# The start of a four-layer attention and gated-MLP kernel: row 0 centred first, row 1's statistics on ScalarE, and three loads moved

## The chip, the cores and the metric

One core of a Trainium2 chip. The kernel is one program, launched once; the metric is its device time in microseconds (us), the median of several runs. A profile of one execution lies beside the times. Its engines are PE (TensorE: matmuls; PEld are its weight loads), DVE (VectorE), ACT (ScalarE), POOL (GpSimd) and SP (SyncE, which here only issues DMAs). "L462" is line 462 of the kernel.

## The reference

The input x has 2048 rows of 576 numbers in bf16. Four residual layers run in turn, A, B, A, B, with the same weights each time:

```
def A(x):                                  # x is already layer-normalised
    q, k, v = split(x @ wqkv)              # 32 heads of 18
    logits = q[s] . k[s - 2 w], w = 0..7   # eight earlier rows, two apart; rows before 0 are masked
    return concat(softmax(logits * 18 ** -0.5) . v) @ wo

def B(x):
    z = gelu(x @ w_in)                     # 576 -> 4608
    z1, z2 = z[:, :2304], layernorm(z[:, 2304:])
    return (z1 * (w_sp @ z2 + b_sp[:, None])) @ w_out

x = x + A(layernorm(x));  x = x + B(layernorm(x));  x = x + A(layernorm(x));  x = x + B(layernorm(x))
```

A layernorm here subtracts the mean of a row and divides by the root of its variance plus 1e-5; it has no weights. Only the start of the first layer A is touched by the change.

## The kernel before

The rows are held in 16 tiles of 128, called rows 0 to 15 below as in the change's name (even and odd positions of the sequence are dealt out to two halves, so that a window's rows are neighbours). For the projections every normalised tile is needed transposed, in `xnT` (128 partitions, 5 chunks of the 576 columns, 2048 rows).

`layer_A` (lines 381 to 939) has a hand order: under a manual schedule the engines PE, ACT, DVE, POOL and SP take their instructions in the order in which the program writes them. For the first layer the start is lines 676 to 817:

- Loads: row 0 on SP and row 1 on ACT's queue, then on SP rows 2 and 3, the weights of v in two halves (`load_wv`), rows 4 to 7, the weights of k and q (`load_wqk`: k first, then q, then k's last 64 columns), and rows 8 to 11, which lie in a spare part of `oT`. Row tiles 12 to 15 follow later (`x3`, line 768), in a buffer that rows 0 to 3 had.
- Before the data is there: a table load for the exponential on ACT, an identity matrix, 46 matmuls on it ("warm"), small constant tables for the attention window (`build_window_rows`, lines 118 to 189), the ones in the last column of `v_ext` (line 703, ACT) and constant borders (`setup_bufs`, POOL).
- Rows 0 to 3, one after the other (lines 750 to 766): statistics on DVE (`B_` two partial statistics, `G_` the aggregate), 1/sqrt in two steps (`R_`: epsilon added on DVE, power on POOL), normalisation on DVE (`A_`), five transposes on PE and a copy by ACT to `xnT` (`T_pe`), and v projections `VW(t, half)`: five matmuls into one PSUM bank, evacuated by ACT into `v_ext`. Attention tile t begins 8 rows ahead of 128 + 120 (t - 1), so tile 1 needs the last 8 rows of row tile 0, tile 2 needs row tiles 1 and 2, tile 3 row tiles 2 and 3.
- Rows 4 to 11 are normalised in groups and transposed by DMA (`T_`, on SP's queue). The window table is written to memory in three small DMAs (`rows[2]` on SP, `rows[3]` on POOL) and read back into `win_pat` by four (`load_pat`, on SP). `fill_window_rows` spreads it over the free partitions of `QK`.
- The first half of the q and k projections (lines 788 to 793): ten steps, (d, cc) with d = 0 to 4 for cc = 0 and again for cc = 1, each with k and q (q alone for d = 4, which holds both). One unit is five matmuls of 512 columns (`PG_mm`, line 462) into one bank, evacuated by ACT into a staging buffer; a full buffer is copied by DMA into `QK` on POOL's and SP's queues. cc = 0 needs rows 0 to 3, cc = 1 rows 4 to 7.
- v projections of tiles 4 to 7, four more units, then the attention steps: logits `L_mm` (line 536), exponential, `PV` (line 559).

Banks of PSUM are taken in turn from a ring of five ("Y", "Y", "PT", "PT", "PT"); one tile more or less moves all that follow by one bank.

Of the kernel before, what the change touches and what calls it, by code (L numbers as in the profile page):

```python
# [18 lines left out]
P = 128  # L19
D = 576  # L20
H = 32
# [42 lines left out]
class K:  # L64
# [131 lines left out]

    def fill_window_rows(self, QK, half):
        nc, n = self.nc, self.cfg.S // 2
        for g0 in (0, 4):
            for a in range(2):  # L200
                nc.vector.tensor_copy(out=QK[:, a, g0:g0 + 4, half * n:(half + 1) * n].rearrange("p g (k x) -> p g k x", x=P),
                                      in_=self.pat[:, a, half, None, None, :].to_broadcast([P, 4, n // P, P]))
            if half == 0:
                nc.vector.tensor_copy(out=QK[:, :, g0:g0 + 4, 0:8], in_=self.pat0[:, :, None, :].to_broadcast([P, 2, 4, 8]))
# [176 lines left out]
    def layer_A(self, li):  # L381
# [46 lines left out]
        def k0_(t):  # L428
            return cfg.tiles[t][2]
# [16 lines left out]

        def VW(t, hh, dve):
            nk = tdim(t)[0]
            pv = self.PT_tile([P, 512], f32, "pv")
            for c in range(5):  # L450
                nc.tensor.matmul(pv[:nk, 0:288], lhsT=self.xnT[:, c, k0_(t):k0_(t) + nk],  # L451
                                 rhs=wv_sb[:, c, hh * 288:(hh + 1) * 288], start=(c == 0), stop=(c == 4))
            evac(v_ext[:nk, t, 16 * hh:16 * hh + 16, 0:DH], pv[:nk, 0:288].rearrange("p (b d) -> p b d", d=DH), dve)

# [221 lines left out]
        if li == 0:  # L676
# [20 lines left out]
            warm = self.PT_tile([P, 512], f32, "warm")  # L697
            for _ in range(46):
                nc.tensor.matmul(warm[:, 0:P], lhsT=self.ident[:], rhs=self.ident[:], start=True, stop=True)
# [3 lines left out]
            nc.scalar.copy(out=v_ext[:, :, :, DH:DH + 1], in_=self.ones[:, None, None, :].to_broadcast([P, NT, H, 1]))  # L703
# [16 lines left out]
            def S_(*tiles):  # L720
                for i in tiles:
                    B_(i)
                    G_(i)

            def R_(i0, n):
                rs = rstds[:, i0:i0 + n]
                nc.vector.tensor_scalar_add(out=rs, in0=mvs[:, i0:i0 + n, 1], scalar1=EPS)
                nc.gpsimd.tensor_tensor(out=rs, in0=rs, in1=self.neg_half[:, 0:1].to_broadcast([P, n]), op=ALU.pow)
            xns = {}
# [7 lines left out]

            def T_pe(i):
                xn = xns.pop(i)
                pt = self.PT_tile([P, 5, P], bf16, "pt")  # L740
                for c in range(5):
                    nc.tensor.transpose(pt[:, c, :], xn[:, c * P:(c + 1) * P], self.ident[:])
                r = i * P
                for c0, c1 in ((0, 3), (3, 5)) if i == 0 else ((0, 5),):
                    nc.scalar.copy(out=self.xnT[:, c0:c1, r:r + P], in_=pt[:, c0:c1])  # L745
# [16 lines left out]
            VW(2, 0, False)  # L762
            T_pe(3)
# [6 lines left out]
            S_(4, 5)  # L770
            R_(4, 2)
            A_(4, 5)
            T_(4, 5)
            S_(6, 7)
            R_(6, 2)
            rows[3](nc.gpsimd)
            A_(6, 7)
            T_(6, 7)
            S_(8)
            self.load_pat(nc.sync)  # L780
            S_(9, 10, 11)
            R_(8, 4)
            S_(12)
            A_(8, 9, 10, 11)
            T_(8, 9, 10, 11)
            self.fill_window_rows(QK, 0)
            S_(13, 14, 15)
# [481 lines left out]
```

## Time and profile before

| | |
|---|---|
| three runs | 1152.56, 1152.94, 1154.53 us; median 1152.94 |
| profiled execution | 1152.74 us, span 1150.9 us |
| PE busy | 1142.6 us of the span |
| DVE, ACT, POOL busy | 539.7, 370.5, 259.6 us |
| first projection matmul (L462) | 13.42 us |
| granted clock of PE | 1.00 throughout |

The profile's page gives the busy time of each engine, the chain of work that ended last, and groups of instructions with the mean duration of one in ns. The timeline gives start, duration, engine, line, operation, what is written from what, and in brackets the idle time before and what ended it; a "q" behind an engine's name is its queue, that is, an issue of a DMA. The view by stretches gives for each stretch the busy time and number of instructions of PE, PEld, DVE, ACT and POOL, then the granted clock, the busy share of the 16 DMA engines and GB/s. Instructions of one engine are pipelined, so neighbours can overlap by some tenths of a us.

### The profile page before, as it was taken

The numbers are of one execution on the slowest core, as the hardware profiler recorded it, in microseconds if no ns is written. First come the engines' busy times: TensorE is split into PE (matmuls) and PEld (weight loads), VectorE is DVE, ScalarE is ACT, GpSimd is POOL, SyncE is SP. The second block draws the span as 40 slices with busy tenths as digits, with TensorE's granted clock in tenths as the row PEclk, the third lists the DMA queues.
The fourth block names the chain that finished last, engine by engine and source line by source line (L and its number), as shares of the span: only waits on it lengthen the run. The fifth ranks groups of instructions, "written<-read, shape, count | busy, mean of one in ns | idle before, by whom it ended". The sixth has DMA issues, their size and how long they took to land.

```text
span 1150.9 us, 29693 instructions
## 1 busy us (share of the span) xinstructions
PE 1142.6 (99%) x12930; PEld 614.5 (53%) x12949; DVE 539.7 (47%) x1198; ACT 370.5 (32%) x660; POOL 259.6 (23%) x387
## 2 busy tenths in 40 slices
PE   8999999999999999999999999999999999999998
PEld 5567554444444444457755775544444444444676
DVE  8789987312233222244466889843322223222312
ACT  5589565011111111102247876541111111011000
POOL 3689654000000000002153767530000000000000
PEclk9999999999999999999999999999999999999999
DMA  8877696000000000049455867920000000001322
GB/s 195 183 164 200 141 211 137 10 13 13 13 1 13 13 13 2 1 152 213 110 110 110 180 152 176 246 60 1 13 13 13 13 13 1 13 2 30 101 74 58
DMA packets 177372, 91.26 MB, mean 79 GB/s; under 512 B 128788, under 2 KB 170420, under 8 KB 177242
## 3 DMA queue, kind: packets, MB, share of 16 engines
q1 hardware_dynamic: 164762, 70.75, 28.1%
q0 software_dynamic: 5888, 12.72, 4.6%
q10 hardware_dynamic: 6592, 5.90, 1.7%
q8 instruction: 101, 1.65, 0.6%
q14 instruction: 29, 0.24, 0.1%
HBM read 35.46 MB, written 14.69 MB: 44 GB/s over the span
## 4 chain that ended last, share of the span: by engine, by line
PE 97%; ACT 1%; DVE 1%; issue 0%; DVEq 0%; ACTq 0%
PE hh L234 79%; PE pp L462 6%; PE pv L451 3%; PE pw L629 3%; PE O_ps L559 3%; PE L_ps L536 2%; ACT P_sb L545 1%; PE L_ps L462 1%; PE hh L1191 0%; PE pt L595 0%; DVE ln_st L715 0%; DVE ln_xn L735 0%; DVE win_bits L158 0%; ACT v_ext L445 0%; ACT xnT L745 0%
## 5 line engine op out<-in xcount | busy, mean ns | idle before, releaser
L234 PE MATMUL hh<-Wq,Z 64*128 64x512 bf16 x4608 | 505.8, 376 | 0.0
L234 PEld LDWEIGHTS <-Z 64*128 64x128 bf16 x6984 | 339.8, 94 | 310.1
L1095 DVE TENSOR_TENSOR g_tmp<-hh,ln_xn 128x512 f32<-128x512 f32 x144 | 92.8, 686 | 452.3 <-PE hh L234 452.3
L947 ACT COPY bank_turn<-ones 1x1 bf16<-1x1 bf16 x239 | 44.8, 188 | 538.5 <-PE hh L234 538.5
L78 POOL DMA_DIRECT2D wout<-in_B_w_out_dram x4 | 4.3, 1075 | 602.0 <-PE hh L234 602.0
L234 PE MATMUL hh<-wout,Z 64*128 64x288 bf16 x2232 | 137.0, 283 | 0.0
L545 ACT ACTIVATE P_sb<-L_ps 128x1440 bf16<-128x1440 f32 (+3 forms) x136 | 125.0, 971 | 24.6 <-PE L_ps L536 23.2
L234 PE MATMUL hh<-xnT,w 64*128 64x512 bf16 x1152 | 132.2, 376 | 0.0
L234 PE MATMUL hh<-win2a,xnT 64*128 64x512 bf16 (+1 forms) x960 | 118.7, 355 | 0.0
L234 PEld LDWEIGHTS <-xnT 64*128 64x128 bf16 x1440 | 69.9, 94 | 70.0 <-issue 0.5
L1020 DVE BATCH_NORM_STATS2 z_st<-zp 128x6 f32<-128x512 bf16 (+1 forms) x160 | 93.0, 624 | 13.0 <-ACT zp L1018 12.9
L1086 ACT ACTIVATE z1T<-hh 128x1024 bf16<-128x1024 f32 x72 | 73.7, 1024 | 61.9 <-PE hh L234 61.9
L234 PEld LDWEIGHTS <-w 64*128 64x128 bf16 x1152 | 56.1, 94 | 68.3
L1096 DVE TENSOR_TENSOR Z<-g_tmp,z1T 128x512 bf16<-128x512 f32 x144 | 92.4, 683 | 0.0
L1018 ACT ACTIVATE zp<-hh 128x1024 bf16<-128x1024 f32 (+1 forms) x96 | 76.1, 810 | 48.8 <-PE hh L234 48.6
L462 PE MATMUL pp<-xnT,wqk_sb 128*128 128x512 bf16 (+1 forms) x313 | 74.2, 379 | 0.9
L234 PE MATMUL hh<-win2b,xnT 64*128 64x512 bf16 (+1 forms) x480 | 72.8, 355 | 0.0
L1160 DVE TENSOR_TENSOR x_new<-hh,xo 128x288 bf16<-128x288 f32 x64 | 26.3, 453 | 93.0 <-PE hh L234 85.0
L299 POOL TENSOR_SCALAR ln_xn<-x_new,ln_mv,ln_rstd 128x576 bf16<-128x576 bf16 x28 | 64.2, 2293 | 2.7
L78 POOL DMA_DIRECT2D QK<-stg x76 | 48.0, 636 | 36.5 <-DVE stg L443 21.9
L462 PEld LDWEIGHTS <-wqk_sb 128*128 128x128 bf16 (+1 forms) x360 | 32.1, 97 | 36.6 <-issue 1.9
L1044 POOL TENSOR_SCALAR Z<-zp,z_mv,z_rstd 128x256 bf16<-128x256 bf16 x32 | 50.7, 1584 | 3.5
(124 smaller groups left out, 753.3 us busy)
## 6 DMA issues: line engine op xcount, KB each, us to landing
xres<-x_new SPq DMA_DIRECT2D x44, 144.0 KB
wout<-in_B_w_out_dram POOLq DMA_DIRECT2D x4, 1296.0 KB, 7.4
xo<-xres SPq DMA_DIRECT2D x32, 144.0 KB
xn_rows<-ln_xn SPq DMA_DIRECT2D x28, 160.0 KB
w<-in_B_w_in_dram SPq DMA_DIRECT2D x16, 256.0 KB
QK<-stg POOLq DMA_DIRECT2D x51, 72.0 KB, 4.4
QK<-stg SPq DMA_DIRECT2D x37, 72.0 KB
xo<-in_A_x_dram SPq DMA_DIRECT2D x6, 288.0 KB
```

The lines of the kernel that those rows point to most:

```text
L78: return eng.dma_start(out=out, in_=in_)
L234: ins = self.nc.tensor.matmul(outs[a_], lhsT=lhs(a_, c, r0), rhs=rhs(a_, c, r0), start=start and k_ == 0, stop=stop and k_ == len(chunks) ...
L299: e.tensor_scalar(out=xn[:nrows, 0:D], in0=x_t[:nrows, :], scalar1=mv[:nrows, 0:1], scalar2=rstd[:nrows, 0:1], op0=ALU.subtract, op1=ALU.mult)
L462: nc.tensor.matmul(pp, lhsT=w, rhs=self.xnT[r0:r1, c, cc * 512:(cc + 1) * 512], start=start, stop=stop, tile_position=(r0, 0))
L545: nc.scalar.activation(out=P_bufs[2 * jp + s % 2][:nk, :, :, 0:nq], in_=Lv[:nk, :, :, 0:nq], func=ACT.Exp, scale=scale)
L947: self.turn_on = lambda tok: nc.scalar.copy(out=tok, in_=self.ones[0:1, 0:1])
L1018: nc.scalar.activation(out=zp[:, w0:w0 + n], in_=pz, func=ACT.Gelu_apprx_tanh)
L1020: nc.vector.bn_stats(out=st[:, x // 512, :], in_=zp[:, x:x + min(512, w0 + n - x)])
L1044: eng.tensor_scalar(out=Z[:, b0:b1, i, :], in0=zv[:, b0:b1, :], scalar1=mv[:, 0:1], scalar2=rstd[:, 0:1], op0=ALU.subtract, op1=ALU.mult)
L1086: lambda ht, z1T=z1T, q2=q2: nc.scalar.activation(out=z1T[:, q2 * 512:(q2 + 2) * 512], in_=ht[:].rearrange("p a b -> p (a b)"), func=ACT.G ...
L1095: nc.vector.tensor_tensor(out=tmp[:], in0=pg[:, a_, :], in1=bsp[:, qs], op=ALU.add)
L1096: nc.vector.tensor_tensor(out=uT(jj)[:, sub, qs], in0=tmp[:], in1=z1Ts[jj, sub][:, qs], op=ALU.mult)
```

## The change

It has these parts.

- Row 0 is centred (mean subtracted, on DVE) right after its statistics, without waiting for 1/sqrt. The centred tile is transposed into a buffer of its own (`o_slots[0]`), and both halves of v's tile 0 are projected from it; ACT multiplies by 1/sqrt when it evacuates them. Row 0 is also normalised and transposed as before, for the rest; its copy to `xnT` is split into the last 8 rows and the first 120.
- Row 1's statistics come from two passes on ACT with an accumulated sum (sum, then squared distance from the mean), with the small steps between them on POOL.
- `VW` is split into its matmuls and its evacuation, and the order on PE becomes: centred row 0, v(0,0), row 0, row 1, v(0,1), v(1,0), row 2, v(1,1), v(2,0), row 3, v(2,1), v(3,0), v(3,1).
- 30 warm matmuls in place of 46; the ones of `v_ext` by POOL, after the power of rows 6 and 7; `setup_bufs`, the clearing of `win_pat` and the write of the first-row table at other places of POOL's order.
- The load of rows 12 to 15 stands on SP behind the transposes of rows 4 to 7.
- `load_pat` is issued by ACT after the first four units of the projections; the fill is split in two, with the normalisation of rows 8 to 11 between, and the statistics of rows 12 to 15 behind.

The diff, cut:

```
-            for _ in range(46):
+            for _ in range(30):
...
-            nc.scalar.copy(out=v_ext[:, :, :, DH:DH + 1], in_=self.ones[:, None, None, :].to_broadcast([P, NT, H, 1]))
             rows[0]()
-            rows[1]()
-            setup_bufs(nc.gpsimd)
...
+            def scaled(out, in_):
+                nc.scalar.activation(out=out, in_=in_, func=ACT.Identity, scale=rstds[:, 0:1])
+            sums = sb.tile([P, 2], f32, name="lnx_sum", tag="lnx_sum", bufs=1)
+            spill = self.xn_bufs[1][:, 0:D]
+            nc.scalar.activation(out=spill, in_=xts[1], func=ACT.Identity, accum_out=sums[:, 0:1])
+            nc.gpsimd.tensor_scalar(out=mvs[:, 1, 0:1], in0=sums[:, 0:1], scalar1=1.0 / D, scalar2=None, op0=ALU.mult)
+            nc.scalar.activation(out=spill, in_=xts[1], func=ACT.Square, scale=-1.0, bias=mvs[:, 1, 0:1],
+                                 accum_out=sums[:, 1:2])
             S_(0)
-            R_(0, 1)
-            for i in range(3):
-                B_(i + 1)
-                A_(i)
-                G_(i + 1)
-                R_(i + 1, 1)
-                T_pe(i)
-                for t, hh in (((0, 0),), ((0, 1),), ((1, 0), (1, 1)))[i]:
-                    VW(t, hh, False)
+            E_(0, 1)
+            xc = self.xn_bufs[0]
+            nc.vector.tensor_scalar(out=xc[:, 0:D], in0=xts[0], scalar1=mvs[:, 0, 0:1], scalar2=None, op0=ALU.subtract)
+            W_(0, 1)
+            B_(2)
+            pt = T_mm(xc)
+            xcT = o_slots[0]
+            for c0, c1 in ((0, 3), (3, 5)):
+                nc.scalar.copy(out=xcT[:, c0:c1], in_=pt[:, c0:c1])
+            scaled(*VW_mm(0, 0, xcT))
+            A_(0)
+            nc.gpsimd.tensor_scalar(out=rstds[:, 1:2], in0=sums[:, 1:2], scalar1=1.0 / D, scalar2=EPS,
+                                    op0=ALU.mult, op1=ALU.add)
+            W_(1, 1)
+            G_(2)
+            E_(2, 1)
+            A_(1)
+            W_(2, 1)
+            rows[1]()
+            pt0 = T_mm(xns.pop(0))
+            T_out(0, pt0, r0=P - 8)
+            pt = T_mm(xns.pop(1))
+            T_out(1, pt)
+            v01 = VW_mm(0, 1, xcT)
+            scaled(*v01)
+            T_out(0, pt0, r1=P - 8)
...
+            v0 = VW_mm(1, 0)
+            pt = T_mm(xns.pop(2))
+            T_out(2, pt)
+            evac(*v0, False)
+            VW(1, 1, False)
+            v0 = VW_mm(2, 0)
+            pt = T_mm(xns.pop(3))
+            T_out(3, pt)
+            evac(*v0, False)
             VW(2, 1, False)
             VW(3, 0, False)
             VW(3, 1, False)
+            rows[3](nc.gpsimd)
+            setup_bufs(nc.gpsimd)
+            S_(4, 5)
+            R_(4, 2)
+            S_(6)
+            A_(4, 5)
+            T_(4, 5)
+            S_(7)
+            R_(6, 2)
+            nc.gpsimd.memset(v_ext[:, :, :, DH:DH + 1], 1.0)
+            A_(6, 7)
+            T_(6, 7)
             x3 = sb.tile([P, 4, D], bf16, name="x_in3", tag="x_in", bufs=2)
             x_load(x3[:], 12, 4, nc.sync)
...
+                if k_ == 1:
+                    self.load_pat(nc.scalar)
+                    self.fill_window_rows(QK, 0, (0,))
+                    A_(8, 9, 10, 11)
+                    T_(8, 9, 10, 11)
+                    self.fill_window_rows(QK, 0, (4,))
+                    S_(12, 13, 14, 15)
```

`E_` is the epsilon add, `W_` the power, `T_mm` the five transposes and `T_out` the copy to `xnT`, `VW_mm` the matmuls of a v unit.

More of the change, by code (lines that the diff above doesn't have):

```diff
@@ L195, in make_ident, with fill_window_rows @@
                                 base=0, pattern=[[-1, P]], channel_multiplier=1)
-    def fill_window_rows(self, QK, half):
+    def fill_window_rows(self, QK, half, g0s=(0, 4)):
         nc, n = self.nc, self.cfg.S // 2
-        for g0 in (0, 4):
+        for g0 in g0s:
             for a in range(2):
@@ L450, in VW @@
             for c in range(5):
[L451 removed]
+                nc.tensor.matmul(pv[:nk, 0:288], lhsT=self.xnT[:, c, k0_(t):k0_(t) + nk] if xT is None else xT[:, c, 0:nk],
                                  rhs=wv_sb[:, c, hh * 288:(hh + 1) * 288], start=(c == 0), stop=(c == 4))
[L453 removed]
+            return v_ext[:nk, t, 16 * hh:16 * hh + 16, 0:DH], pv[:nk, 0:288].rearrange("p (b d) -> p b d", d=DH)
+        def VW(t, hh, dve):
+            evac(*VW_mm(t, hh), dve)
         stg_tiles, stg_left = {}, {}
@@ L742, in T_pe, with T_out @@
                     nc.tensor.transpose(pt[:, c, :], xn[:, c * P:(c + 1) * P], self.ident[:])
-                r = i * P
-                for c0, c1 in ((0, 3), (3, 5)) if i == 0 else ((0, 5),):
-                    nc.scalar.copy(out=self.xnT[:, c0:c1, r:r + P], in_=pt[:, c0:c1])
+                return pt
+            def T_out(i, pt, c0=0, c1=5, r0=0, r1=P):
+                nc.scalar.copy(out=self.xnT[:, c0:c1, i * P + r0:i * P + r1], in_=pt[:, c0:c1, r0:r1])
             def T_(*tiles):
```

40 lines of the change are left out of this document (15 added, 25 removed).

## The prediction

> **What bounds the kernel now.** I read the page's busy shares first, then the chain of waits of the first 60 us in order of time, then the timeline of the first 45 us.
>
> ```profile
> PE 1142.6 (99%) x12930; PEld 614.5 (53%) x12949; DVE 539.7 (47%) x1198; ACT 370.5 (32%) x660; POOL 259.6 (23%) x387
> ```
> ```profile
> 3.00 0.98 DVE win_bits L158 x4
> ...
> 8.81 0.45 PE pt L742 x5
> 9.26 1.85 PE pv L451 x15
> ...
> 13.85 10.74 PE pp L462 x49
> ...
> 33.01 4.90 PE pv L451 x40
> ```
>
> TensorE (PE) is busy for 99% of the span, and from 13.42 us, where the first q/k projection (line 462) starts, the chain is PE on PE: 10.74 / 49 = 0.219 us a matmul, then 4.90 / 40 = 0.1225 us a matmul of the v projection. Nothing in the change alters what PE does after that point. So the change is worth what it does to the start of the first projection, plus any stall that it plants later. The whole start-up is 13.4 us, 1.2% of the time. The profiled execution took 1152.74 us around a span of 1150.9 us; it lies 0.2 us under the median of the three runs (1152.94).
>
> The start-up itself, by the timeline (start, duration, engine, what):
>
> ```profile
> 1.36 3.99 PE L699 MATMUL warm<-ident 128*128 128x128 bf16 x46 [1.36 <-POOL ident L194]
> 2.58 2.53 ACT L703 COPY v_ext<-ones 128x544 bf16<-128x544 bf16 x1
> 3.39 0.54 POOL L163 MEMSET win_pat<- 128x528 bf16 x1
> 3.56 0.82 DVE L715 BATCH_NORM_STATS2 ln_st<-x_in 128x6 f32<-128x288 bf16 x2
> 4.66 0.15 DVE L727 TENSOR_SCALAR lnx_rstd<-lnx_mv 128x1 f32<-128x1 f32 x1
> 4.73 0.81 DVE L715 BATCH_NORM_STATS2 ln_st<-x_in 128x6 f32<-128x288 bf16 x2
> 4.90 0.58 POOL L728 TENSOR_TENSOR lnx_rstd<-lnx_rstd,neg_half 128x1 f32<-128x1 f32 x1 [0.23 <-DVE lnx_rstd L727]
> 5.51 0.43 DVE L735 TENSOR_SCALAR ln_xn<-x_in,lnx_mv,lnx_rstd 128x576 bf16<-128x576 bf16 x1
> 6.00 0.45 PE L742 MATMUL pt<-ident,ln_xn 128*128 128x128 bf16 x5 [0.65 <-DVE ln_xn L735]
> 6.49 0.75 ACT L745 COPY xnT<-pt 128x384 bf16<-128x384 bf16 x2 [1.38 <-PE pt L742]
> 7.03 0.79 PE L451 MATMUL pv<-wv_sb,xnT 128*128 128x288 bf16 x5 [0.57 <-ACT xnT L745]
> 7.65 0.44 PE L742 MATMUL pt<-ident,ln_xn 128*128 128x128 bf16 x5
> 7.93 0.78 PE L451 MATMUL pv<-wv_sb,xnT 128*128 128x288 bf16 x5
> 11.43 0.70 ACT L745 COPY xnT<-pt 128x640 bf16<-128x640 bf16 x1
> 12.18 1.40 PE L451 MATMUL pv<-wv_sb,xnT 128*128 128x288 bf16 x10 [0.19 <-ACT xnT L745]
> 13.42 19.59 PE L462 MATMUL pp<-xnT,wqk_sb 128*128 128x512 bf16 x88
> ```
>
> From these rows I take three prices. A v unit (five matmuls) holds PE 0.62 us (7.03 to 7.65). A block of five transposes holds PE 0.28 us (7.65 to 7.93). From the start of a transpose to the first matmul that can use it are 1.22 us: 0.45 for the transposes, a copy of 0.70 and about 0.07 of handing over; for row 0, whose copy is split, 1.03 (6.00 to 7.03). In 6.00 to 13.42 PE's work is 4 x 0.28 + 8 x 0.62 = 6.1 us; the other 1.3 us are such waits.
>
> **The change, part by part.**
>
> *Row 0 centred first.* Now VectorE (DVE) waits for GpSimd's power (4.90 to 5.48) before it normalises at 5.51. After, the subtraction of the mean follows the epsilon add directly, in the place where row 1's statistics stand at 4.73; at the same 0.43 us it ends at 5.16, and the transposes start at 5.16 + 0.06 = 5.22 instead of 6.00: **0.78 us earlier**. In exchange row 0 is transposed a second time (normalised, for the projections): +0.28 us on PE, and row 0's copy is redone as 8 and 120 columns.
>
> *What PE then waits for.* The hand order of PE is now: centred row 0, v(0,0), row 0, row 1, v(0,1), v(1,0), row 2, v(1,1), v(2,0), row 3, v(2,1), v(3,0), v(3,1). Step by step: transposes 5.22; v(0,0) at 5.22 + 1.03 = 6.25 to 6.87; row 0 to 7.15; row 1 to 7.43; v(0,1) to 8.05. v(1,0) needs row 1's copy, 7.15 + 1.22 = 8.37, to 8.99. Row 2 to 9.27; v(1,1) to 9.89. v(2,0) needs row 2's copy, 8.99 + 1.22 = 10.21, to 10.83; row 3 to 11.11; v(2,1) to 11.73; v(3,0) needs row 3's copy, 10.83 + 1.22 = 12.05; two units, and the projections start at 12.05 + 1.24 = **13.3**, against 13.42. The order puts one v unit between a transpose and its use; 0.28 + 0.62 covers 0.90 of 1.22 us, so 0.32 is lost three times. Before it was lost once, ahead of 12.18, since v(1,0), v(1,1), v(2,0) ran as 15 matmuls without a gap (the chain, at 9.26). The head start of 0.78 is thus spent: 0.28 on the extra transposes and about 0.4 on the two new waits. DVE's rows are in time: all of them move up, because row 1's statistics (0.81 us) have left DVE.
>
> *Row 1's statistics on ScalarE (ACT).* Two passes over 128x576 and, between them, a small op on GpSimd. The nearest rows:
>
> ```profile
> L293 ACT ACTIVATE ln_xn<-x_new,ln_nmr,ln_rstd 128x576 bf16<-128x576 bf16 x15 | 13.0, 868 | 62.3 <-POOL bank_turn L1130 59.0 <-POOL ln_nmr L283 3.3
> L283 POOL TENSOR_SCALAR ln_nmr<-ln_mv,ln_rstd 128x1 f32<-128x1 f32 x15 | 4.0, 266 | 1.5
> ```
>
> So 2 x 0.87 + 0.27 + 0.2 of handing over = 2.2 us from the landing of row 1. Behind the second pass in ACT's order stand the copies of the centred row (ready at 5.71) and then every evacuation; behind GpSimd's mean stands row 0's power, first needed at 5.8. The trace does not show when row 1 lands. It bounds it: by 4.73, when its statistics run now, and hardly ahead of row 0, read at 3.56. At 3.56 the passes end at 5.76, 0.05 late; at 4.73 at 6.93, 1.2 late. I take 3.56, the row of the equal load, and keep 1.2 as the bad end. The accumulating form could also be dearer than 0.87; that works as a later landing.
>
> *Fewer warm-up matmuls, and the ones.* 46 become 30, about 1.4 us less on PE while it waits for row 0 anyway: nothing. The copy of the ones (2.53 us on ACT, 2.58 to 5.11) makes room for the statistics; on GpSimd it stands behind the power of rows 6 and 7, priced between 0.54 (as many contiguous elements, L163) and 2.53 (the same strided tile on ACT). I take 2.5, as the tile is the same. Beside it stands the normalisation of rows 6 and 7, which has until the second half of the projections, ten units of 1.09 after the start less one: 13.3 + 9 x 1.09 = 23.1.
>
> *Pads and buffers moved off GpSimd's early queue.* The pads at 3.39 to 3.93 stand beside four DVE ops on 3 elements that end only at 3.98. Without them row 0's statistics could start up to 0.2 us sooner: -0.2 is the good end, 0 what I take, since row 0's landing may hold them. The Trainium skill, "SBUF — State Buffer", section "Who interferes with whom", says GpSimd and a DVE op in a two-port mode exclude each other for a whole instruction; the stretched ops agree. By it the ones could hold back the normalisation of rows 6 and 7 for their whole length.
>
> *Transposes ahead of the load of rows 12 to 15; pattern load on ACT.*
>
> ```profile
> 12.49 1.45 SPq L78 DMA_DIRECT2D x_in<-in_A_x_dram  x1
> 14.03 6.20 SPq L306 DMA_TRANSPOSE xnT<-ln_xn  x4
> 17.87 0.76 POOL L78 DMA_DIRECT2D win_period<-win_first  x1 [0.31 <-POOL win_first L182]
> 21.81 1.60 SPq L78 DMA_DIRECT2D win_pat<-win_period  x4
> 23.51 5.17 SPq L306 DMA_TRANSPOSE xnT<-ln_xn  x4
> 24.71 2.36 DVE L201 COPY QK<-win_pat 128x4096 bf16<-128x4096 bf16 x2 [0.39 <-DMA win_pat<-win_period]
> 36.60 6.45 SPq L78 DMA_DIRECT2D QK<-win2a  x8
> 48.14 0.40 PE L536 MATMUL L_ps<-QK 32*128 32x128 bf16 x16
> ```
>
> SP's four transposes lose the 1.45 us load ahead of them; they end by about 19 instead of 20.2, needed at 23.1: no gain on PE. Rows 12 to 15 are read after 25 us. The pattern goes out after the fourth evacuation, near 18.4, and holds ACT for 1.6 us; its wait, the write of the first-row table (issued about 10.5, 3.9 us to land, as 17.87 to 21.81), is over by 15. Behind it stand the evacuations, but five PSUM banks turn, so PE first needs a held bank at the tenth unit, 13.3 + 9 x 1.09 = 23.1: 3 us of cover, each us beyond would cost one. The fill then starts near 21.4 instead of 24.71. Rows 8 to 11 are normalised after the first fill, so their transposes start near 24.3 instead of 23.51 and SP's later copies move up to 1 us back: the last at 44 instead of 43.05 (36.60 + 6.45), first used by the second logits at 48.1. Covered, no gain, since nothing on PE waits for them now.
>
> **Sum:** 1152.74 - 0.78 + 0.28 + 0.4 (waits) + 0.05 (statistics) = 1152.7 us; with the 0.2 us to the median, **1152.8**: no change.
>
> **Rivals.**
>
> *Late statistics* (slower within 0.2%): row 1 lands at 4.73 or the accumulating passes cost over 1.2 us each. Copies 0.6 to 1.2 us late: 1153.4 to 1154.0. For it: the 16 DMA engines are full at 3 to 4 us (1.08 of them in the first row below). Against: at its 356 GB/s the 0.15 MB of a row takes 0.4 us.
>
> ```profile
> 3.00:4.00 1.00, 1.00 (x13) 1.00 (x10) 1.00 (x7) 1.00 (x1) 1.00 (x10) 1.00 1.08 356
> 0.00:12.00 12.00, 9.30 (x96) 7.71 (x96) 10.60 (x46) 8.26 (x13) 6.08 (x35) 1.00 0.89 257
> ```
> ```profile
> L699 PE MATMUL warm<-ident 128*128 128x128 bf16 x46 | 4.0, 270 | 1.4 <-POOL ident L194 1.4
> L699 PE MATMUL warm<-ident 128*128 128x128 bf16 x4 | 0.6, 306 | 0.0
> L699 PE MATMUL warm<-ident 128*128 128x128 bf16 x6 | 0.5, 221 | 0.0
> ```
>
> *A cold PE* (the other side, slower by over 0.2%). The three rows are the warm-up matmuls: all of them, those running in 3.8 to 3.9 us, those in 4.2 to 4.3. A matmul drops from 306 to 221 ns around 4.1 us, though the granted clock (the figure 1.00 of the rows by stretch) does not show it. With a mean of 270 over 46, some 26 were slow, in 4.1 - 1.36 = 2.7 us or 105 ns apart, so 30 leave four, 0.4 us of margin. If the speed-up comes later than 4.5 us in an execution, the warm-up ends without it and the thin start-up work runs at half speed: 5 x 0.28 + 8 x 0.62 = 6.4 us more if all of it does. I price it at 2.5 us, some 40% of that: **1155.2**. Against: PE is busy up to 4.5 us as before. The Trainium skill, "TensorE: Matmul & The Clock Gate", section "What's actually happening", gives a free-running window of about 3.4 us of activity; by it 30 x 105 ns = 3.15 us might miss one, and the trace's 2.7 us shows that a full window was not needed here.
>
> *A full head start* (faster, within 0.2%): the copies run quicker than I chain them, or statistics start 0.2 earlier and row 1 lands early. The bound is the weights of q: rows 0 to 7, the v weights, k's and q's are 3.1 MB in the order of SP's queue, and 12.0 us at 257 GB/s have moved 3.1 MB. With 1.3 us to land (23.41 to 24.71 for the pattern) the second unit cannot start before 13.3, the first not before 12.2: at most -1.2, 1151.7.
>
> *Late rows 6 and 7*: the ones take over 5 us or SP is held, and the second half waits at 23.1; 1 to 3 us, 1154 to 1156.
>
> **How the numbers follow.** Forecast (within 0.6 us of 1152.8) 0.56, late statistics 0.14, full head start 0.13, cold PE 0.09, late rows 0.04 (three quarters of it beyond 0.2%), something unseen that makes it faster 0.04. What a measurement of this kernel can tell from no change is about 0.2%, 2.3 us (the three runs lie 2.0 us apart). Faster by more 0.05, within 0.83, slower by more 0.12. The range reaches from the head start's bound, a little under for scatter, to the late statistics' 1154.0 and part of the cold case: 1151.5 to 1154.8.
>
> **What would show it.** In the changed kernel's timeline: first transposes near 5.2, a gap of 0.3 us before v(1,0), v(2,0) and v(3,0), first projection between 13.0 and 13.6, and no PE gap at 23 or 48 us. Wrong if the first copy starts well after 5.7, if the v units' matmuls are 0.24 us apart, if the first projection starts before 12.5, or if PE waits for a bank near 23 us.

## The result, and the profile after

The changed kernel takes 1157.29 us (median of six runs, 1156.17 to 1158.72); the kernel before, run beside it on the same chip, 1152.8 us (six runs, 1152.56 to 1154.53). The ratio is 1.0038, with a 95% interval of 1.0025 to 1.0051: 4.4 us slower. Forecast were 1152.8 us and no change, with 1154.8 as the upper end.

The profiled execution of the changed kernel took 1158.56 us around a span of 1156.8, 5.8 us more than that of before. The page of it, the busy share of PE:

```profile
PE 1147.7 (99%) x12938; PEld 614.0 (53%) x12938; DVE 541.1 (47%) x1195; ACT 370.4 (32%) x665; POOL 263.9 (23%) x390
```

PE was busy for 5.1 us more. This alone does not tell slow matmuls from waits: the change issues 11 matmuls fewer (16 warm ones out, five transposes in; the weight loads, PEld, fell by just 11, from 12949 to 12938), but 8 more are on record (12938 against 12930), so about 19 that went unrecorded in the profile of before are counted as busy here. The timeline tells it. Two stretches of it answer to the rows shown of before. The start (start, duration, engine, what):

```profile
...
3.77 0.68 ACT L761 ACTIVATE ln_xn<-x_in 128x576 bf16<-128x576 bf16 x1 [1.09 <-DMA x_in<-in_A_x_dram]
4.36 0.19 ACT L761 ACTIVATION_READ_ACCUMULATOR ln_xn<-x_in 128x1 f32 x1
4.93 0.77 ACT L763 ACTIVATE ln_xn<-x_in,lnx_mv 128x576 bf16<-128x576 bf16 x1 [0.38 <-POOL lnx_mv L762]
...
5.16 0.71 PE L747 MATMUL pt<-ident,ln_xn 128*128 128x128 bf16 x5 [0.42 <-DVE ln_xn L768]
6.45 1.38 PE L451 MATMUL pv<-wv_sb,o_slot 128*128 128x288 bf16 x5 [0.57 <-ACT o_slot L774]
...
10.89 0.44 PE L747 MATMUL pt<-ident,ln_xn 128*128 128x128 bf16 x5
...
15.20 9.01 PE L465 MATMUL pp<-xnT,wqk_sb 128*128 128x512 bf16 x41
```

Row 0's transposes start at 5.16 instead of 6.00, as forecast. But five of them take 0.71 instead of 0.45 us and the first v unit 1.38 instead of 0.79; only the transposes at 10.89 have the old length. PE runs at about half speed until 10 us, and the first projection starts at 15.20 instead of 13.42: 1.8 us lost. (The line numbers are those of the changed kernel: L465 is the projection that was L462, L539 the logits that were L536, L741 the normalisation that was L735.)

The stretch behind it:

```profile
16.09 2.45 POOL L820 MEMSET v_ext<- 128x544 bf16 x1
16.18 2.86 DVE L741 TENSOR_SCALAR ln_xn<-x_in,lnx_mv,lnx_rstd 128x576 bf16<-128x576 bf16 x2 [0.81 <-POOL lnx_rstd L730]
...
19.88 2.10 ACTq L78 DMA_DIRECT2D win_pat<-win_period  x4
...
24.73 2.36 DVE L201 COPY QK<-win_pat 128x4096 bf16<-128x4096 bf16 x2 [1.73 <-DMA win_pat<-win_period]
...
27.21 1.44 DVE L741 TENSOR_SCALAR ln_xn<-oT,lnx_mv,lnx_rstd 128x576 bf16<-128x576 bf16 x4
...
27.66 5.30 SPq L306 DMA_TRANSPOSE xnT<-ln_xn  x4
33.05 8.48 SPq L78 DMA_DIRECT2D QK<-stg  x9
41.64 7.53 SPq L78 DMA_DIRECT2D QK<-win2a  x8
...
43.94 0.34 PE L539 MATMUL L_ps<-QK 32*128 32x128 bf16 x11
46.09 0.23 PE L539 MATMUL L_ps<-QK 32*128 32x128 bf16 x3 [1.80 <-DMA QK<-win2a]
46.82 0.23 PE L539 MATMUL L_ps<-QK 32*128 32x128 bf16 x2 [0.50 <-DMA QK<-stg]
46.98 6.18 PE L465 MATMUL pp<-xnT,wqk_sb 128*128 128x512 bf16 x20
...
54.32 0.40 PE L539 MATMUL L_ps<-QK 32*128 32x128 bf16 x16
```

Of before, four rows of the same stretch that were not shown yet:

```profile
22.87 1.45 DVE L735 TENSOR_SCALAR ln_xn<-oT,lnx_mv,lnx_rstd 128x576 bf16<-128x576 bf16 x4 [0.20 <-POOL lnx_rstd L728]
...
28.79 7.71 SPq L78 DMA_DIRECT2D QK<-stg  x9
...
42.16 0.40 PE L536 MATMUL L_ps<-QK 32*128 32x128 bf16 x16
42.49 4.49 PE L462 MATMUL pp<-xnT,wqk_sb 128*128 128x512 bf16 x19
```

Read from the end: the second logits start at 54.32 instead of 48.14, 6.2 us late, and behind them the two profiles run nearly alike (their spans differ by 5.9). Of these 6.2 us, 1.8 are the start. The first logits begin at 43.94 (42.16 + 1.78) and then wait 1.80 + 0.50 us for copies into `QK`; before, all 16 ran without a gap, and the projections behind them began at 42.49, here at 46.98: 2.7 more. Those twenty projections take 6.18 instead of 4.49 us: 1.7 more.

Why the copies are late, SP's rows tell. Rows 8 to 11 are normalised at 27.21, right behind the first half of the fill, instead of 22.87; SP's transposes of them start at 27.66 instead of 23.51; behind those stand SP's copies of the staging buffers (33.05 instead of 28.79) and of win2a (41.64 instead of 36.60). The chain of waits says the same in order of time (start, duration, what):

```profile
39.12 7.57 DMA QK<-stg
...
46.82 0.23 PE L_ps L539 x2
```

The last copy that the first logits need leaves SP's queue at 39.1 and lands 7.6 us later. And why the projections are slow, the view by stretches tells (the eighth figure, before the DMA share and GB/s, is PE's granted clock; it is 1.00 in the stretches before and after these):

```profile
48.00:49.00 1.00, 1.00 (x5) 0.40 (x3) 0.77 (x3) 1.00 (x2) 0.00 (x0) 0.61 0.54 178
49.00:50.00 1.00, 1.00 (x3) 0.30 (x2) 1.00 (x2) 0.07 (x1) 0.00 (x0) 0.50 0.35 100
50.00:51.00 1.00, 1.00 (x4) 0.40 (x3) 1.00 (x2) 0.59 (x1) 0.00 (x0) 0.50 0.54 111
51.00:52.00 1.00, 1.00 (x5) 0.39 (x4) 1.00 (x2) 0.00 (x0) 0.00 (x0) 0.68 0.49 99
```

The missing clock adds up to 0.39 + 0.50 + 0.50 + 0.32 = 1.71 us, that is, half speed for 3.4 us; it is the 1.7 us of the projections. The Trainium skill, "TensorE: Matmul & The Clock Gate", section "What's actually happening", has the clock at half after at least one idle window of about 3.4 us and back at full after a busy window of that length, with windows that run free. The trace agrees with the half, and with the length of the busy window that ends it. The waits ahead of the fall were 2.3 us in all, with a few matmuls among them, less than such an idle window; no run here shows where the windows lie.

The theory is that SP's late copies, behind rows 8 to 11, make the loss; its rival is that the start makes it, by a clock that 30 matmuls do not raise in time. A third suspect showed up beside them. So three things were to be told apart: the order of rows 8 to 11 against the fill, the 30 warm matmuls, and the ones on GpSimd, which run 2.45 us and beside which the normalisation of rows 6 and 7 takes 2.86 instead of 0.78 us.

### The profile page after: what moved, and what is told of

It reads as the page before. It is cut to its first block, busy times and chain, and to the rows that moved or that the text cites. A ratio compares the mean times of both kernels' runs of the same rounds, so it can differ in the third digit from the quotient of the medians.

```text
span 1156.8 us, 29698 instructions
## 1 busy us (share of the span) xinstructions
PE 1147.7 (99%) x12938; PEld 614.0 (53%) x12938; DVE 541.1 (47%) x1195; ACT 370.4 (32%) x665; POOL 263.9 (23%) x390
## 4 chain that ended last, share of the span: by engine, by line
PE 98%; DMA 1%; ACT 1%; issue 0%; DVE 0%; SPq 0%; DVEq 0%; ACTq 0%
PE hh L234 79%; PE pp L465 6%; PE pv L451 3%; PE pw L632 3%; PE O_ps L562 3%; PE L_ps L539 2%; DMA QK<-stg 1%; PE L_ps L465 1%; ACT P_sb L548 1%; PE hh L1238 0%; PE pt L598 0%; DMA x_in<-in_A_x_dram 0%; PE pt L747 0%; ACT xnT L751 0%; SPq L78 0%
## 5 line engine op out<-in xcount | busy, mean ns | idle before, releaser
L465 PE MATMUL pp<-xnT,wqk_sb 128*128 128x512 bf16 (+1 forms) x330 | 77.1, 385 | 0.0
L78 POOL DMA_DIRECT2D QK<-stg x76 | 49.2, 650 | 35.4 <-DVE stg L443 22.4
L465 PEld LDWEIGHTS <-wqk_sb 128*128 128x128 bf16 (+1 forms) x360 | 32.6, 98 | 37.7 <-issue 4.2
```

The source lines that it names most:

```text
L78: return eng.dma_start(out=out, in_=in_)
L465: nc.tensor.matmul(pp, lhsT=w, rhs=self.xnT[r0:r1, c, cc * 512:(cc + 1) * 512], start=start, stop=stop, tile_position=(r0, 0))
```

## The experiments

**46 warm matmuls in the changed kernel.**

```
-            for _ in range(30):
+            for _ in range(46):
```

> The changed kernel with 46 warm-up matmuls again. Theory: two causes, a clock that is still low in the start (about 1.8 us, as the first projection stands at 15.20 instead of 13.42 us in the profile) and copies into QK that are late for the first logits (about 4 us with what follows). The 46 take away the first cause alone: first projection near 13.4 us, first logits still waiting 2 us or more, about 1155.4 us. Rival: the number of warm-up matmuls is not what kept the clock low, and the thin chain after them or chance did; then the first projection stays near 15 us and the time near 1157.3 us.

Measured: 1156.83 us (1155.49 to 1157.94, five runs), ratio 1.0036 [1.0023, 1.0048]. The first projection starts at 13.61, 1.6 us earlier than in the profile above, as the theory had it, and yet only 0.5 us is gained: the time missed the theory's 1155.4 and lies nearer to the rival's 1157.3. The first logits begin at 42.35 and wait 0.53 and 0.62 us for the same copies (2 us or more were expected), since these hang on SP and not on PE; 1.35 us more are lost at 54.86 to the transposes of rows 12 to 15, the next in SP's queue. A start that comes earlier only waits longer: the copies set the time.

**Rows 8 to 11 ahead of the whole fill.** The normalisation and transposes are written ahead of the projections' loop, so that they stand ahead of the fill; all else is the changed kernel.

```
             S_(8, 9, 10, 11)
             R_(8, 4)
+            A_(8, 9, 10, 11)
+            T_(8, 9, 10, 11)
...
                     self.fill_window_rows(QK, 0, (0,))
-                    A_(8, 9, 10, 11)
-                    T_(8, 9, 10, 11)
                     self.fill_window_rows(QK, 0, (4,))
```

> The changed kernel with rows 8 to 11 normalised and transposed ahead of the pattern load and the fill, as before the change; nothing else. Theory: SP's transposes then start near 24.6 us instead of 27.66, its copies into QK follow 3 us sooner, the first logits no longer wait and the clock does not fall there; the first projection stays near 15 us: about 1154 us (1153.5 to 1155). Rival: the copies are late because the pattern lands late (load on ACT, beside the load of rows 12 to 15) and all copies wait for the fill; then the first logits still wait over 1.5 us and the time stays above 1156 us.

Measured: 1153.80 us (1153.24 to 1154.23, 11 runs), ratio 1.0008 [0.9999, 1.0016]: 3.5 of the 4.4 us are back. The timeline:

```profile
24.35 5.17 SPq L306 DMA_TRANSPOSE xnT<-ln_xn  x4
...
42.22 0.40 PE L539 MATMUL L_ps<-QK 32*128 32x128 bf16 x16
...
49.31 0.21 PE L539 MATMUL L_ps<-QK 32*128 32x128 bf16 x1 [0.36 <-DMA QK<-win2a]
```

The transposes start 3.3 us earlier, the first logits no longer wait, and the clock stays at 1.00. One matmul of the second logits still waits. One thing came otherwise than expected: with the same 30 warm matmuls the clock was up in time in this profile, and the first projection starts at 13.48, not near 15.

**Both together.** The two edits above in one kernel.

> Both of the above: 46 warm-up matmuls, and rows 8 to 11 ahead of the fill. Theory: both causes gone, first projection near 13.4 us, no wait of the first logits over 0.6 us, 1152.6 us (1152 to 1153.3), within 0.1% of the kernel before. Rivals: if the warm-up is not the cause, 1154 us as with the rows alone; if the order of rows 8 to 11 is not, 1155.4 us as with the warm-up alone.

Measured: 1154.60 us (1153.69 to 1155.49, 11 runs), ratio 1.0016 [1.0007, 1.0025]. This missed: 1.7 us are left, so order and warm-up are not all. The 46 matmuls did not even help: the time is 0.8 us above that with the order alone, near the rival's 1154 ("if the warm-up is not the cause"). In its profile the start is at full clock (first projection 13.61), the first logits run without a wait, and the second wait 0.73 us for copies of win2a.

**30 warm matmuls in the kernel before.**

```
-            for _ in range(46):
+            for _ in range(30):
```

> The kernel before with 30 warm-up matmuls instead of 46 and nothing else. Theory: its start loses the raised clock too; first projection 1 to 2 us later, no new wait at the first logits: about 1154.3 us. Rival (the warm-up count plays no part): 1152.8 us, first projection at 13.4 us.

Measured: 1154.13 us (1152.54 to 1155.81, 11 runs), ratio 1.0008 [1.0000, 1.0017]. Two runs lie at 1152.5 to 1152.9, nine at 1153.9 to 1155.8. The profile is of the lowest run: clock raised in time, transposes of 0.45 us, first projection at 13.18, 0.24 us before that of before. So fewer warm matmuls can gain 0.2 us or lose 1 to 3, from run to run. The median is the theory's, but that a late clock makes the nine slower runs is not shown: none of them was profiled.

**The kernel before with rows 8 to 11 between the halves of the fill.** The one part alone.

```
-            A_(8, 9, 10, 11)
-            T_(8, 9, 10, 11)
-            self.fill_window_rows(QK, 0)
+            self.fill_window_rows(QK, 0, (0,))
+            A_(8, 9, 10, 11)
+            T_(8, 9, 10, 11)
+            self.fill_window_rows(QK, 0, (4,))
```

> The kernel before with one thing moved: rows 8 to 11 are normalised and transposed between the two halves of the fill, as in the changed kernel; start-up, warm-up, ones and pattern load as before. Theory (the order of rows 8 to 11 against the fill is the cause): the pattern lands at 24.7 us, so the normalisation starts near 27.1 and SP's transposes near 27.6 instead of 23.51; the last staging copies that the first logits need land 18 to 19 us after that, 45.5 to 47, and the first logits, due at 42.2, lose 2.5 to 4 us: 1155.5 to 1157.5, with a PE wait ending on QK<-stg. Rival (the new start or the ones on GpSimd cause it, and the order alone is covered by slack): 1152.9, no PE wait at 42 to 47.

Measured: 1157.57 us (1156.77 to 1157.82, five runs), ratio 1.0035 [1.0021, 1.0049]: the whole loss of the change, from this edit alone, at the upper end of what the theory expected (1157.5). Its timeline:

```profile
25.16 2.36 DVE L201 COPY QK<-win_pat 128x4096 bf16<-128x4096 bf16 x2 [2.47 <-DMA win_pat<-win_period]
...
28.10 5.35 SPq L306 DMA_TRANSPOSE xnT<-ln_xn  x4
...
45.49 0.47 PE L536 MATMUL L_ps<-QK 32*128 32x128 bf16 x13 [1.76 <-DVE stg L443]
45.89 4.49 PE L462 MATMUL pp<-xnT,wqk_sb 128*128 128x512 bf16 x20
```

DVE stands idle for 2.47 us at 22.7, with rows 8 to 11 ready to be normalised behind the fill in its queue. PE then loses 1.2 us to a staging buffer, 1.76 at the first logits (a wait that ends with DVE's evacuation into a staging buffer, not with a copy) and 1.0 at the second. In this execution the clock does not fall (20 projections in 4.49 us), and the loss is waits alone. That its size is the change's 4.4 us is in part chance: there the waits are shorter and the clock falls.

**The new start alone.** The changed kernel's start with 46 warm matmuls and the ones on GpSimd, and behind it the order of before; the edit of the changed kernel, cut:

```
+            x3 = sb.tile([P, 4, D], bf16, name="x_in3", tag="x_in", bufs=2)
+            x_load(x3[:], 12, 4, nc.sync)
...
             nc.gpsimd.memset(v_ext[:, :, :, DH:DH + 1], 1.0)
             A_(6, 7)
             T_(6, 7)
+            S_(8)
+            self.load_pat(nc.sync)
+            S_(9, 10, 11)
             R_(8, 4)
+            S_(12)
+            A_(8, 9, 10, 11)
+            T_(8, 9, 10, 11)
+            self.fill_window_rows(QK, 0)
...
-                    self.load_pat(nc.scalar)
```

> The changed kernel's start up to the v projections (row 0 centred, row 1's statistics on ScalarE, new order on PE, ones on GpSimd) with 46 warm matmuls, and behind it the order of before: load of rows 12 to 15 ahead of the transposes, pattern load on SP, rows 8 to 11 ahead of the whole fill. Theory (the start is neutral and the whole loss lies in the order behind it): first projection at 13.6 and the total within 0.5 us of before, 1152.7 to 1153.4; the ones still hold back the normalisation of rows 6 and 7 by 2 us, and the transposes of rows 8 to 11 start 0.5 to 1 late. Rival (the new start costs by itself what the runs with rows 8 to 11 put first still lack): 1154 to 1154.8.

Measured: 1155.26 us (1154.27 to 1156.69, 11 runs), ratio 1.0016 [1.0007, 1.0024]. The theory expected at most 1153.4, the rival at most 1154.8, so both missed. The profile shows two things. The clock was raised late in that execution, so that the 46 warm matmuls themselves held the transposes until 5.86 (first projection 13.94). And the ones beside the normalisation of rows 6 and 7 (2.86 us again) stand ahead of SP's transposes of rows 8 to 11, which start at 25.73, 2.2 us after those of before (0.5 to 1 was expected); the second logits wait 0.89 + 0.36 us for win2a. That pointed at the ones.

**The ones behind the power of row 8**, so that they run beside statistics.

```
             R_(6, 2)
-            nc.gpsimd.memset(v_ext[:, :, :, DH:DH + 1], 1.0)
             A_(6, 7)
...
-            S_(8, 9, 10, 11)
-            R_(8, 4)
+            S_(8)
+            R_(8, 1)
+            nc.gpsimd.memset(v_ext[:, :, :, DH:DH + 1], 1.0)
+            S_(9, 10, 11)
+            R_(9, 3)
```

The kernel is otherwise that of both edits together. The edit does two things: the ones move, and row 8 gets its power by itself, ahead of that of rows 9 to 11.

> The run with 46 warm matmuls and rows 8 to 11 first, with the ones on GpSimd moved behind the power of row 8, so that they run beside statistics and not beside the normalisation of rows 6 and 7. Theory (the memset blocks the normalisation, and this makes SP's chain about 1 us late, for which the second logits wait): that normalisation falls from 2.86 to 0.78 us, the transposes of rows 8 to 11 start near 23.5, and the second logits' wait of 0.7 us on QK<-win2a goes: 1153.2 to 1153.6 against 1154.6. Rival (the load of rows 12 to 15 and the pattern load on ScalarE's queue delay the copies by themselves): 1154.3 to 1154.8.

Measured: 1153.30 us (1152.54 to 1153.72, 11 runs), ratio 1.0001 [0.9992, 1.0009]: the time of before. The same kernel with the ones in the old place was 1.7 us above the kernel before run beside it; by the bare medians of the two the gain is 1.3 us. The timeline of this one, and of both edits one row:

```profile
16.11 0.77 DVE L741 TENSOR_SCALAR ln_xn<-x_in,lnx_mv,lnx_rstd 128x576 bf16<-128x576 bf16 x2 [0.81 <-POOL lnx_rstd L730]
...
18.61 2.47 POOL L827 MEMSET v_ext<- 128x544 bf16 x1
18.93 0.77 DVE L715 BATCH_NORM_STATS2 ln_st<-oT 128x6 f32<-128x288 bf16 x2
...
20.98 0.43 DVE L741 TENSOR_SCALAR ln_xn<-oT,lnx_mv,lnx_rstd 128x576 bf16<-128x576 bf16 x1
...
21.44 5.20 SPq L306 DMA_TRANSPOSE xnT<-ln_xn  x4
...
48.41 0.40 PE L539 MATMUL L_ps<-QK 32*128 32x128 bf16 x16
```
```profile
24.00 1.45 DVE L741 TENSOR_SCALAR ln_xn<-oT,lnx_mv,lnx_rstd 128x576 bf16<-128x576 bf16 x4 [1.13 <-POOL lnx_rstd L730]
```

The normalisation takes 0.77 us again. The same memset, now beside the statistics of row 9, leaves these at their 0.77 us. SP's transposes start at 21.44, 2 us ahead of before, and nothing waits at the logits. The Trainium skill, "SBUF — State Buffer", section "Who interferes with whom", has it that a DVE instruction outside its two-port modes with one input does not contend with GpSimd. The row of the statistics agrees with it, if they are such an instruction, which no run here shows by itself.

The transposes were expected near 23.5, so this is 2 us more than the theory's. The normalisation of row 8 starts at 20.98, where with both edits that of rows 8 to 11 starts at 24.00 and has waited 1.13 us for the power of all four. So of the 3.0 us the ones make about 1.9 and the power of row 8 about 1.1; no run parts the two. With the 1.9 alone the transposes would start near 22.6, still ahead of before.

**Pattern load back on SP.** Again the kernel of both edits.

```
-            S_(8, 9, 10, 11)
+            S_(8)
+            self.load_pat(nc.sync)
+            S_(9, 10, 11)
...
-                    self.load_pat(nc.scalar)
```

> The run with 46 warm matmuls and rows 8 to 11 first, with the pattern load back on SP's queue behind the statistics of row 8; the ones stay where the change put them. Theory (the ones are what is left): SP issues four small DMAs near 21.5 as before and the transposes of rows 8 to 11 still start at 24.4, the second logits still wait: 1154.3 to 1154.8. Rival (the four issues of 3.5 us on ScalarE hold back its evacuations and so the staging copies): ScalarE keeps up, copies move up by up to 1 us, 1153.0 to 1153.8.

Measured: 1155.57 us (1153.68 to 1157.58, ten runs), ratio 1.0021 [1.0012, 1.0030]. No gain from freeing ScalarE, which speaks against the rival; it lies above the theory's 1154.8 too. The transposes of rows 8 to 11 start at 25.32 here, and the clock was raised later than in any other profile with 46. The group of the 46 warm matmuls (busy time, mean ns) shows it, this kernel first, then the one of both edits:

```profile
L702 PE MATMUL warm<-ident 128*128 128x128 bf16 x46 | 5.1, 313 | 1.4 <-POOL ident L194 1.4
```
```profile
L702 PE MATMUL warm<-ident 128*128 128x128 bf16 x46 | 4.3, 284 | 1.4 <-POOL ident L194 1.4
```

With a mean of 313 ns none of the 46 ran fast, and the transposes waited for them until 6.24. The same instructions had a mean of 270 in before, 277 in the kernel before with the order changed, 284 in the kernel of both edits.

**The mended order with the change's 30 warm matmuls.** The kernel with the ones moved, and `range(30)`.

> The run with rows 8 to 11 first and the ones behind the power of row 8, with the change's 30 warm matmuls in place of 46. Theory (with 30 the clock is raised before row 0's transposes in some executions and near 10 us in others): first projection at 13.4 to 13.6 us in a warm execution and near 15.2 in a cold one, times of 1152.5 to 1154.8 spread wider than the 1.2 us of the run with 46, median 0.3 to 1.2 above it. Rival (30 cost nothing once the order is mended): median 1153.0 to 1153.4 and a spread of about 1.2 us.

Measured: 1153.19 us (1152.58 to 1154.38, 11 runs), ratio 1.0001 [0.9992, 1.0010]. The median missed the theory: it is not above that of 46. The spread is 1.8 us, with seven runs up to 1153.5 and four at 1153.9 to 1154.4, which a late clock in some of them would make; no profile of one of the four exists. In the profile the transposes at 5.11 are still slow (0.72 us), the v unit at 6.39 is fast, and the first projection starts at 13.46.

**12 warm matmuls in the kernel before**: the suspected cost made large.

```
-            for _ in range(46):
+            for _ in range(12):
```

> The kernel before with 12 warm matmuls, all over by 2.7 us: the suspected cost made large. Theory (what the warm-up buys is the clock at the first transposes): the 5 x 0.28 + 8 x 0.62 us of transposes and v projections run at half speed wholly or in part, first projection between 14.5 and 17 us, transposes near 310 ns and v matmuls near 440 ns each until the clock is raised, total 1154.5 to 1157. Rival (the start-up work raises the clock by itself within a microsecond, or the loads bound the start anyway): first projection by 13.6, total 1153 to 1153.5.

Measured: 1154.98 us (1154.14 to 1155.53, 11 runs), ratio 1.0016 [1.0007, 1.0025]. The timeline of it:

```profile
6.02 0.71 PE L742 MATMUL pt<-ident,ln_xn 128*128 128x128 bf16 x5 [3.21 <-DVE ln_xn L735]
7.30 1.38 PE L451 MATMUL pv<-wv_sb,xnT 128*128 128x288 bf16 x5 [0.57 <-ACT xnT L745]
...
13.14 0.44 PE L742 MATMUL pt<-ident,ln_xn 128*128 128x128 bf16 x5
```

The start-up work runs slow until some point between 11 and 13 us, and the whole costs 2.0 us in the median: that is the price of a start without the clock, and about all that a warm-up can buy here.

**The changed kernel, a second profile.**

> The changed kernel itself, a second profile. Theory (the moment at which the clock is raised differs from one execution to the next): transposes of row 0 at 5.1 to 5.4 us, and either again 310 ns each and the first projection near 15.2, or 220 ns and 13.5; in both the first logits wait for the staging copies, and the total is 1156 to 1158.7. Rival (the slow clock at the start belongs to this kernel, by its matmuls and waits): slow again until about 10 us.

Measured: one run, 1159.42 us. Its timeline:

```profile
5.17 0.72 PE L747 MATMUL pt<-ident,ln_xn 128*128 128x128 bf16 x5 [0.43 <-DVE ln_xn L768]
6.46 0.79 PE L451 MATMUL pv<-wv_sb,o_slot 128*128 128x288 bf16 x5 [0.57 <-ACT o_slot L774]
...
7.64 0.78 PE L451 MATMUL pv<-wv_sb,o_slot 128*128 128x288 bf16 x5
8.59 0.79 PE L451 MATMUL pv<-wv_sb,xnT 128*128 128x288 bf16 x5 [0.17 <-ACT xnT L751]
...
13.53 0.81 PE L465 MATMUL pp<-xnT,wqk_sb 128*128 128x512 bf16 x3
...
23.84 2.36 DVE L201 COPY QK<-win_pat 128x4096 bf16<-128x4096 bf16 x2
...
45.41 0.23 PE L539 MATMUL L_ps<-QK 32*128 32x128 bf16 x3 [2.30 <-DMA QK<-win2a]
46.45 0.23 PE L539 MATMUL L_ps<-QK 32*128 32x128 bf16 x2 [0.81 <-DMA QK<-win2a]
46.61 6.18 PE L465 MATMUL pp<-xnT,wqk_sb 128*128 128x512 bf16 x20
```

This time the transposes were still slow (0.72 us), but the clock was raised by the first v unit, and the first projection starts at 13.53: a mixture of the theory's two cases, and not the rival's slow start until about 10 us. The execution is not shorter for it: the first logits wait 3.1 us instead of 2.3, and the 20 projections behind them again take 6.18 us, with a granted clock of 0.50 from 47 to 50 us. The total of 1159.42 lies above the 1158.7 expected; 1.07 us of the excess is a pause of PE at 63.85 that nothing in the profile explains.

The profiles side by side, by the start of SP's transposes of rows 8 to 11 (PE's waits at the logits, in us, summed from the timeline; all end with a copy into `QK` but the 0.34 and the 1.76, which end with an evacuation by DVE into a staging buffer; the profiles left out show none):

| kernel | transposes | first logits | second logits |
|---|---|---|---|
| ones later | 21.44 | 0 | 0 |
| before | 23.51 | 0 | 0 |
| rows first | 24.35 | 0 | 0.36 |
| both | 24.46 | 0 | 0.73 |
| pattern on SP | 25.32 | 0.34 | 0.83 |
| new start alone | 25.73 | 0 | 1.25 |
| changed, 46 warm | 26.43 | 1.15 | 0.18 |
| changed, second profile | 26.79 | 3.11 | 0 |
| changed | 27.66 | 2.30 | 0 |
| before, fill first | 28.10 | 1.76 | 1.01 |

The kernel before has less than a microsecond of slack here: from 24.35 on the second logits wait for copies, and from about 26 on the first as well.

## Why the prediction was wrong, point by point

- *Row 0 centred first*: right. Transposes at 5.22 forecast, 5.16 and 5.17 measured. With 46 warm matmuls these themselves hold them until 5.53 to 6.24.
- *What PE then waits for*: right, in sum and in parts. Where the clock was up by the first v unit, the unit behind a wait starts 0.95 us after the one ahead of it (8.59 and 7.64 in the second profile), that is 0.62 of work and 0.33 lost, where 0.32 were forecast; the 0.17 in brackets counts from the modelled end of the matmuls before. From the first v unit to the first projection are 7.07 us, 7.04 forecast. What is off is where the first v unit starts: at 6.39 to 6.55 instead of 6.25 in these profiles, since transposes at 5.11 or 5.17 still ran slow (5.17 to 6.46 is 1.29, not 1.03) and fast ones started at 5.40 or later. Five such profiles of this start have the first projection at 13.46 to 13.61, against 13.0 to 13.6 forecast; a sixth, with the ones moved, has 13.70. The head start is worth nothing, as the sum had it. (By its own terms the sum is 1152.9, not 1152.8; nothing hangs on it.)
- *Row 1's statistics on ScalarE*: right. The row is there at 3.77 at the latest, the second pass's sum is read by 5.80, and the copy of the centred row starts at 5.91, when the slow transposes end. Each pass needs a second instruction of 0.19 us to read the sum, which the price of 2.2 us left out, but the passes are shorter (0.68 and 0.77): 2.03 us in all.
- *Fewer warm-up matmuls: nothing*: wrong in part of the executions. The rival of a cold PE had 0.09 and a price of 2.5 us; measured are 1.7 (15.20 against 13.53) and 2.0 with hardly any warm-up. The margin of 0.4 us came from a single profile; the moment of the raise lies at 4.1 us there and after 6.2 in another. Yet this is not what made the changed kernel slow: with 46 it is hardly faster, and its second profile had the clock and no gain.
- *The ones on GpSimd*: the price was right (2.45 against 2.5) and so was the block that the prediction weighed. The consumer was wrong. Rows 6 and 7 were indeed in time for 23.1, but the 2.1 us move everything behind them in DVE's queue, the statistics of rows 8 to 11 and their transposes. Moving them, together with the early power of row 8, gained 0.7 us with 30 warm matmuls and 1.7 with 46 once the order was mended, each kernel taken against the kernel before run beside it.
- *Pads off GpSimd's queue*: right as taken, 0. Row 0's statistics start at 3.58, with the pads gone, when its load lands.
- *Pattern load on ScalarE*: mis-sized. Issuing takes 2.10 us instead of 1.6, the pattern lands 2.75 us after that, and DVE is busy with statistics until 23.0; the fill starts at 24.73, not 21.4. In the second profile the pattern was there in time, and the fill starts at 23.84, right behind the statistics. The ring of banks did cover ScalarE: no wait of PE near 23 us.
- *Rows 8 to 11 behind the first fill*: **the step that failed.** It read: "their transposes start near 24.3 instead of 23.51 and SP's later copies move up to 1 us back: the last at 44 instead of 43.05, first used by the second logits at 48.1. Covered, no gain, since nothing on PE waits for them now." The start was 27.66, not 24.3, and SP's last copy into `QK` left at 49.2. The forecast let the fill start when the pattern lands and did not count what stands ahead of it in DVE's queue, the statistics of rows 8 to 11, which the ones hold back by 2.1 us; in the first profile 1.7 us of waiting for the pattern come on top. With SP that late, the first logits already wait for its copies, not only the second. Shown by the edit alone in the kernel before (+4.3 us) and by its undoing in the changed one (-3.5 us). The second half of the step failed too, but by little: with rows 8 to 11 first the transposes start at 24.35, just where the forecast had them, and the second logits wait 0.36 us. That nothing waits now was no proof of slack; the slack was under a microsecond at the second logits.
- *The falling clock* behind the stall was in no part of the sum. In both profiles of the changed kernel it costs 1.7 us, on top of the 2.3 and 3.1 us of waiting. The runs that were not profiled speak for it too: the mean granted clock of a run is below 1.000 in five of six timed runs of the changed kernel and in four of five of the kernel before with the order changed (its profiled run, with 1.76 us of waiting at the first logits, is the fifth), in none of the 22 runs of the two kernels with rows 8 to 11 first and the ones in their old place, and in the others in one or two runs each. But the runs with the fall are not always the slower ones (1156.77 to 1157.82 with it and 1157.57 without it in the kernel before with the order changed), so what it costs in the end is open. Which stall makes it fall was not tried further.

Of the 4.4 us the order explains 3.5 (the fall of the clock included) and the ones, with the power of row 8, most of the rest: with 30 warm matmuls 0.9 us are left over the kernel before with the order mended, and 0.2 with the ones moved too. What the 30 warm matmuls add is between nothing (in the mended kernel) and 1.3 us (in before) and stays open for the changed kernel by itself, where the waiting hides it. No version beats the kernel before: with everything mended and row 0's transposes 0.9 us earlier, time is as before (1.0001).

## What to carry to other kernels

Ask of every step that moves back in an in-order queue what stands behind it, follow that to its first consumer on the busy engine, and measure the slack there (landing against need); that nobody waits for it now may mean less than 1 us of slack, as here, or much more. An early instruction whose data is late holds back ready work behind it, so what is ready goes first, and a GpSimd memset of some length belongs beside DVE's statistics, not beside its scalings. Before cutting a warm-up, look at several profiles: the moment of the clock's raise differs from run to run, and an idle stretch of 2 to 3 us may cost another 1.7 us in clock.

## What the runs showed of the hardware

- The clock's raise after the first matmul at 1.36 us came after 2.7 us (before) and after no less than 4.8 us (46 warm matmuls, none fast) in kernels whose first matmuls are the same.
- After a stall the granted clock was 0.50 for 3.4 us, twice, and the fall came 0.2 and 1.2 us after the projections had started again (reckoned from the granted clock of the stretch it falls into); at the start the slow matmuls (310 ns) are seen in their length alone, while the granted clock reads 1.00.
- A GpSimd memset of 128x544 strided elements takes 2.45 us and holds a DVE scaling of bf16 for its length (2.86 instead of 0.78 us), but not the partial statistics (0.77 us beside it).
- An accumulating activation over 128x576 is two instructions, 0.68 to 0.77 us and 0.19 us to read the sum.
- Issuing the four small DMAs of the pattern took ScalarE 1.81 to 3.56 us in the profiles (2.10 in the changed kernel's) and SP 1.60 to 1.72.
